# Sums of the down projection moved ahead of the activation's last product on VectorE

## The chip, the core and the metric

The kernel runs on one core of a Trainium2 chip. The metric is the device time of one execution in microseconds (us). TensorE (PE) multiplies matrices into PSUM; VectorE (DVE), ScalarE (ACT) and GpSimd (POOL) work on tiles; SyncE (SP) issues most DMAs. Each engine runs its own instructions strictly in the order in which the program lists them, and semaphores make one wait for another.

## The reference

An attention with a learned bias on relative position feeds a first feed-forward layer with the activation h cos(h), which feeds a second, gated layer behind an RMS norm. Only the first feed-forward layer ("layer 1") matters here:

```python
def _moe_ref(x, w_in, w_out) -> np.ndarray:
    h = x @ w_in              # x: 2304 x 512, w_in: 512 x 2048
    g = h * np.cos(h)
    return (g @ w_out).astype(np.float32)
```

## The kernel before

**Precision.** Every float32 factor of layers 1 and 2 is held as a pair, a rounded first half and a second half with the rest, and `mm3` forms each product from three matmuls (first times first, first times second, second times first). So a weight or an activation is usable only when both halves are written: ScalarE copies the first half, POOL then subtracts it from the value for the second.

**Items.** Layer 1 cuts the 2304 tokens into five blocks `BLKS` (four of 512 and one of 256 columns, block 2) and the 2048 hidden features into 16 groups f of 128. Four groups are one chunk c. An item is one (chunk, block, f); items run chunk by chunk, in a chunk block by block, in a block over its four f. Chunks 0 to 2 take the blocks in the order 0, 1, 2, 3, 4, the last chunk in the order 0, 2, 1, 3, 4. That is 80 items, 20 for each chunk; layer 2 follows with items 80 to 139.

**An item.** `run_item(n)` emits the up product and activation of item n (`item_up`), then the down product of item n-2 (`item_down`, the lag is `LAG`), then `w_tick`. In `item_up` TensorE makes h in one of three PSUM tiles of tag h. VectorE reduces h to the range of the sine (L544 to L546: t, t, r), does half of a weight conversion (`w_fill`: L114 and L115, or L118 and L119), and ScalarE takes the absolute value and the sine of r (L549, L550). VectorE's last step is the product t = r * h (L551); ScalarE copies g's first half from t (L552), POOL makes its second half (L553).

**Down.** `item_down` adds g times the weight into four PSUM tiles y of tag "y", of which there are five. When the last of a block's four f is through (fi == 3), VectorE empties the four tiles into the accumulator `yacc` (`yaccs` for the block of 256 columns): a copy in chunk 0 (L598), a sum later (L600). The next block's down product, one item later, has one spare tile; for its second tile it waits for the first of those four steps.

**Weights.** A weight piece is loaded by DMA, converted from its 64-bit form by VectorE in two halves (`w_fill`), and split into two halves wA or wB by ScalarE (L132) and POOL (L133), in `w_split`. `w_tick` emits at most one split at the end of an item of layer 1, as soon as the buffer's last use has been emitted. The split after item 21 is that of the up weight which item 23 is the first to use; after items 41 and 61 likewise for items 43 and 63.

Of the kernel before, what the change touches and what calls it, by code (L numbers as in the profile page):

```python
# [7 lines left out]
F32 = mybir.dt.float32  # L8
# [3 lines left out]
ALU = mybir.AluOpType  # L12
# [33 lines left out]
def attn_moe(tc, qd, kd, vd, smallp, lrow, ident_d, wf1, wf2, rmsg, out):  # L46
    nc = tc.nc
# [89 lines left out]
    def w_fill(halves=1):  # L137
        for _ in range(halves):
            if wstate["conv"] < wstate["absd"]:
                w_conv()  # L140

    def w_tick(can_split, nsplit=1):

        for _ in range(nsplit):
            i = wstate["split"]
            if i < wstate["convd"] and can_split(i):
                w_split()
        i = wstate["abs"]
        if i < wstate["dmad"] and i < wstate["splitd"] + NW32:
            w_abs()  # L150
        while wstate["dma"] < NP and wstate["dma"] < wstate["conv"] + NRAW:
            w_dma()
        for k in ("dma", "abs", "conv", "split"):
            wstate[k + "d"] = wstate[k]
# [111 lines left out]
    for i, T in enumerate(TORDER):  # L266
# [3 lines left out]
        if nT <= 512 and i % 5 > 1:  # L270
            ps = psA.tile([128, 512], F32, tag="tr", name="psb", bufs=3)
        else:
            ps = psB.tile([128, 1024], F32, tag="S", name="psb", bufs=2)
# [235 lines left out]
    def up(wt, bi, name):  # L509
        t0, tn = BLKS[bi]  # L510
        ps = psH.tile([128, 512], F32, tag="h", name=name, bufs=3)
        mm3(ps[:, :tn],
            [(wt[:, 0, 128 * c:128 * c + 128], wt[:, 1, 128 * c:128 * c + 128],
              xh[:, c, t0:t0 + tn], xl[:, c, t0:t0 + tn]) for c in range(4)],
            tn, True, True)
        return ps
# [3 lines left out]
    def tasks(n, fns):  # L520
        k = 0
        for fn, *a in later.get(n, ()):
            if fn in fns:
                fn(*a)
                k += 1
        return k

    def fill(n):
        return tasks(n, (rms_add, rms_mean, rms_xn))

    def item_up(n):
        m, c, bi, fi = items[n]
        t0, tn = BLKS[bi]
        f = c * (CH1 if m == 1 else CH2) + fi
        g = mp.tile([128, 2, 512], F32R, tag="g", name="g", bufs=LAG + 2)
        if n == 0:

            mp.tile([128, 40], F32, name="even")
        if m == 1:
            ps = up(w_t[(1, f, 0)], bi, "h")[:, :tn]  # L540
            tasks(n, (rms_sum, rms_back))
            t = mp.tile([128, 512], F32, tag="t", name="t", bufs=2)[:, :tn]
            r = mp.tile([128, 512], F32, tag="r", name="r", bufs=2)[:, :tn]
            nc.vector.tensor_scalar(t, ps, INV2PI, MAGIC, op0=ALU.mult, op1=ALU.add)  # L544
            nc.vector.tensor_scalar(t, t, MAGIC, -TWO_PI, op0=ALU.subtract, op1=ALU.mult)  # L545
            nc.vector.tensor_tensor(r, ps, t, op=ALU.add)  # L546
            if fill(n) < WF:
                w_fill()
            nc.scalar.activation(r, r, AF.Abs)  # L549
            nc.scalar.activation(r, r, AF.Sin, bias=halfpi[:, 0:1], scale=-1.0)  # L550
            nc.vector.tensor_tensor(t, r, ps, op=ALU.mult)  # L551
            nc.scalar.copy(g[:, 0, :tn], t)  # L552
            nc.gpsimd.tensor_tensor(g[:, 1, :tn], t, g[:, 0, :tn].bitcast(F32), op=ALU.subtract)  # L553
        else:
            pg = up(w_t[(2, f, 0)], bi, "hg")[:, :tn]
            tasks(n, (rms_sum, rms_back))
            t = mp.tile([128, 512], F32, tag="t", name="t", bufs=2)[:, :tn]
            nc.scalar.activation(t, pg, AF.Sigmoid)  # L558
            nc.vector.tensor_tensor(t, t, pg, op=ALU.mult)  # L559
            fill(n)  # L560
            pv = up(w_t[(2, f, 1)], bi, "hv")[:, :tn]
            nc.vector.tensor_tensor(t, t, pv, op=ALU.mult)  # L562
            nc.scalar.copy(g[:, 0, :tn], t)  # L563
            nc.gpsimd.tensor_tensor(g[:, 1, :tn], t, g[:, 0, :tn].bitcast(F32), op=ALU.subtract)  # L564
        gt[n] = g

    def item_down(n):
        m, c, bi, fi = items[n]
        t0, tn = BLKS[bi]
        ch = CH1 if m == 1 else CH2  # L570
        nch = (NF1 if m == 1 else NF2) // ch
        f = c * ch + fi
        g = gt.pop(n)
        wt = w_t[(m, f, 1 if m == 1 else 2)]
        nd = 4 if m == 1 else tn // 128
        wid = tn if m == 1 else 512
        if fi == 0:
            ypsum[bi] = [env["psY"].tile([128, 512], F32, tag="y", name="y", bufs=5) for _ in range(nd)]
        for d in range(nd):
            ps = ypsum[bi][d][:, :wid]  # L580
            w_ = (wt[:, 0, 128 * d:128 * d + 128], wt[:, 1, 128 * d:128 * d + 128], g[:, 0, :tn], g[:, 1, :tn])
            if m == 1:
                mm3(ps, [w_], tn, fi == 0, fi == ch - 1)
            else:
                gs = slice(128 * d, 128 * d + 128)
                mm3(ps, [(g[:, 0, gs], g[:, 1, gs], wt[:, 0, :], wt[:, 1, :])], 512, fi == 0, fi == ch - 1)
        if fi == ch - 1:
            acc = yacc if m == 1 else oacc
            if c == 0:
                if tn == 512:  # L590
                    acc[bi] = env["yp"].tile([128, 4, 512], F32, tag="y", name="yacc", bufs=4)
                else:
                    acc[bi] = env["yp"].tile([128, nd, wid], F32, tag="ys", name="yaccs", bufs=1)
            a = acc[bi]
            for d in range(nd):
                ps = ypsum[bi][d][:, :wid]
                if c == 0:
                    nc.vector.tensor_copy(a[:, d, :wid], ps)  # L598
                else:
                    nc.vector.tensor_tensor(a[:, d, :wid], ps, a[:, d, :wid], op=ALU.add)  # L600
                if m == 2 and c == nch - 1:
                    nc.sync.dma_start(out[t0 + 128 * d:t0 + 128 * d + 128, :], a[:, d, :])
            if m == 1 and c == nch - 1:
                return bi
        return None
# [63 lines left out]
    def ready(i):  # L669
        while wstate["split"] <= i:  # L670
            if wstate["split"] < wstate["conv"]:
                w_split()
            elif wstate["conv"] < wstate["abs"]:
                w_conv()
            elif wstate["abs"] < wstate["dma"]:
                w_abs()
            else:
                w_dma()

    def run_item(n):  # L680
        tasks(n, (rms_sq, rms_out))
        if n < NI:
            m, c, bi, fi = items[n]
            ready(pieces.index((m, c * (CH1 if m == 1 else CH2) + fi, m - 1)))
            item_up(n)
        d = n - LAG
        if d >= 0:
            m, c, bi, fi = items[d]
            ready(pieces.index((m, c * (CH1 if m == 1 else CH2) + fi, m)))
            bi = item_down(d)  # L690
            if bi is not None:
                n0 = NI1 + RMS_AT[ORDER2.index(bi)]
                for i, x in enumerate(RMS_STEPS):
                    later.setdefault(n0 + i, []).extend((x_[0], bi, *x_[1:]) for x_ in x)
        m, c, bi, fi = items[min(n, NI - 1)]
        w_tick(lambda i: i < WA + WB or lastuse[pieces[i - WA - WB]] <= n - SPL,
               nsplit=2 if n < 6 or m == 2 else 1)
        if m == 2:
            w_fill(2 if n % 2 else 1)
# [6 lines left out]
    for i in range(6):  # L706
        w_split(nc.vector if i % 2 == 0 else nc.gpsimd)
    w_tick(lambda i: False)
    run_item(0)
    av(15, 1, [0, 1, 2, 3, 4])  # L710
    norm_out(15, 1)
    run_item(1)
    st_psA.close()
    st_ap.close()
# [4 lines left out]
    for n in range(2, NI + LAG):  # L719
        run_item(n)  # L720
# [70 lines left out]
```

## Time and profile before

| | us |
|---|---|
| median of 3 runs | 1206.61 (1205.63 to 1207.86) |
| the profiled execution, its own time | 1208.49 |
| its span, first to last instruction | 1206.7 |
| PE busy | 1181.8 (98%) |
| DVE busy | 832.5 (69%) |
| ACT busy | 537.9 (45%) |
| POOL busy | 350.2 (29%) |
| layer 1 up to the turn to layer 2, 350 to 800 us: PE busy | 442.30 of 450.00 |

The granted clock of TensorE is 0.999 of full speed over the span. Matmul ends in the trace are modelled, so a pause of TensorE is best read from the starts before and after it. In a row of the timeline the first number is the start in us from the span's start, the second how long the row lasts; "x4" merges four instructions; a bracket gives the engine's idle time just before and what ended it.

### The profile page before, as it was taken

To read this page: it belongs to the slowest core of one execution; us is meant where nothing else is said; L and a number is where in the kernel's file an instruction comes from. 1 tells how busy PE (TensorE), PEld (TensorE's weight loads), DVE (VectorE), ACT (ScalarE), POOL (GpSimd) and SP (SyncE) were. 2 spreads that over 40 slices of the span, in tenths; PEclk is the share of its full clock that TensorE was granted. 3 is DMA by queue.
4 is the path that set the end of the run, shared out by engine and by line. 5 is a ranking of instruction groups with operands and counts; after the bars stand their busy time and mean duration, and the time that the engine had idled before them with its cause. 6 is when DMAs were issued, how large, how long until landed. Compare 5 with 4: busy or idle time off the path is not lost.

```text
span 1206.7 us, 17433 instructions
## 1 busy us (share of the span) xinstructions
PE 1181.8 (98%) x6596; PEld 907.8 (75%) x6596; DVE 832.5 (69%) x1593; ACT 537.9 (45%) x1073; POOL 350.2 (29%) x356
## 2 busy tenths in 40 slices
PE   7899999999999999999999999999999999999998
PEld 2266666666668888878888877878888888888887
DVE  8866677777669988879878988786456255633232
ACT  6866666666655444445434546422322132222111
POOL 4001011010124234225224445663331242124111
PEclk9999999999999999999999999999999999999999
DMA  5842516343001211201111101111012011200012
GB/s 159 272 158 73 172 34 190 101 133 118 12 1 53 69 37 53 71 18 53 53 35 36 53 18 35 37 53 53 26 45 70 18 35 53 71 1 1 35 43 80
DMA packets 30324, 79.26 MB, mean 66 GB/s; under 512 B 3873, under 2 KB 4129, under 8 KB 30241
## 3 DMA queue, kind: packets, MB, share of 16 engines
q1 hardware_dynamic: 29616, 76.09, 20.1%
q0 software_dynamic: 480, 1.77, 0.6%
q8 instruction: 52, 0.85, 0.3%
q10 hardware_dynamic: 144, 0.29, 0.1%
q14 instruction: 32, 0.25, 0.1%
HBM read 62.52 MB, written 15.61 MB: 65 GB/s over the span
## 4 chain that ended last, share of the span: by engine, by line
PE 84%; DVE 10%; ACT 3%; issue 1%; DMA 1%; POOL 0%; DVEq 0%; ACTq 0%
PE y L506 24%; PE h L506 13%; PE hg L506 11%; PE hv L506 11%; PE o L370 7%; PE psS L313 6%; PE pt L343 5%; PE rp L389 2%; DVE ft L248 2%; PE psS L318 2%; PE psb L277 2%; DVE t L545 1%; DVE yacc L600 1%; PE pt L353 1%; DVE r L546 1%
## 5 line engine op out<-in xcount | busy, mean ns | idle before, releaser
L506 PE MATMUL y<-g,wB 128*128 128x512 f32 (+1 forms) x960 | 214.1, 370 | 5.2 <-DVE yacc L600 1.7
L506 PEld LDWEIGHTS y<-g,wB 128*128 128x128 f32 x960 | 167.7, 188 | 38.7 <-DVE yacc L600 3.0
L553 POOL TENSOR_TENSOR g<-t,g 128x512 fp32r<-128x512 f32 (+1 forms) x80 | 97.4, 1217 | 236.7 <-ACT g L552 236.7
L564 POOL TENSOR_TENSOR g<-t,g 128x512 fp32r<-128x512 f32 (+1 forms) x60 | 74.3, 1239 | 292.1 <-ACT g L563 292.1
L506 PE MATMUL h<-xh,wB 128*128 128x512 f32 (+1 forms) x480 | 145.4, 369 | 0.0
L506 PE MATMUL y<-wB,g 128*128 128x512 f32 x594 | 143.6, 389 | 0.0
L327 DVE CUSTOM_DVE_ANT_0 e<-psS,bias 128x576 f32<-128x576 f32 x144 | 103.7, 754 | 46.5 <-PE psS L313 31.4
L506 PE MATMUL hv<-xh,wB 128*128 128x512 f32 (+1 forms) x440 | 133.6, 369 | 0.0
L506 PE MATMUL hg<-xh,wB 128*128 128x512 f32 (+1 forms) x440 | 133.2, 368 | 0.4 <-DVE t L559 0.4
L559 DVE TENSOR_TENSOR t<-t,hg 128x512 f32<-128x512 f32 (+1 forms) x60 | 38.0, 633 | 137.5 <-ACT t L558 137.5
L331 ACT ACTIVATE e<-e,sm 128x576 f32<-128x576 f32 x144 | 110.6, 769 | 42.9 <-DVE sm L327 42.8
L506 PEld LDWEIGHTS y<-wB,g 128*128 128x128 f32 x594 | 110.8, 188 | 22.5
L558 ACT ACTIVATE t<-hg 128x512 f32<-128x512 f32 (+1 forms) x60 | 33.3, 554 | 168.0 <-PE hg L506 161.7
L563 ACT CAST g<-t 128x512 fp32r<-128x512 f32 (+1 forms) x60 | 34.7, 578 | 164.6 <-DVE t L562 164.6
L549 ACT ACTIVATE r<-r 128x512 f32<-128x512 f32 (+1 forms) x80 | 47.1, 589 | 124.3 <-DVE r L546 123.9
L506 PEld LDWEIGHTS h<-xh,wB 128*128 128x128 f32 x480 | 87.8, 188 | 15.9 <-issue 0.5
L370 PE MATMUL o<-eT,v 128*64 128x256 f32 (+1 forms) x640 | 93.5, 413 | 0.0
L506 PEld LDWEIGHTS hg<-xh,wB 128*128 128x128 f32 x440 | 80.5, 188 | 15.0 <-DVE t L559 0.9
L506 PEld LDWEIGHTS hv<-xh,wB 128*128 128x128 f32 x440 | 80.6, 188 | 13.7
L506 PE MATMUL h<-xl,wB 128*128 128x512 f32 (+1 forms) x240 | 88.4, 368 | 0.0
L133 POOL TENSOR_TENSOR wB<-w,wB 128x512 fp32r<-128x512 f32 x58 | 83.1, 1441 | 0.3 <-ACT wB L132 0.3
L552 ACT CAST g<-t 128x512 fp32r<-128x512 f32 (+1 forms) x80 | 46.2, 578 | 81.3 <-DVE t L551 76.7
(116 smaller groups left out, 2142.7 us busy)
## 6 DMA issues: line engine op xcount, KB each, us to landing
raw<-in_wf_dram SPq DMA_DIRECT2D x68, 512.0 KB, 3.6
bflat<-G SPq DMA_DIRECT2D x36, 295.5 KB, 4.0
bias<-bflat SPq DMA_DIRECT2D x26, 288.0 KB, 2.9
kt<-in_kd_dram SPq DMA_DIRECT2D x16, 320.0 KB, 4.2
qt<-in_qd_dram SPq DMA_DIRECT2D x16, 320.0 KB, 4.5
v<-in_vd_dram SPq DMA_DIRECT2D x16, 320.0 KB, 3.8
out_dram<-yacc SPq DMA_DIRECT2D x16, 256.0 KB, 2.1
bias<-bflat POOLq DMA_DIRECT2D x6, 288.0 KB, 5.7
```

What stands on the lines that cost most here:

```text
L133: eng.tensor_tensor(t[:, 1, :], r, t[:, 0, :].bitcast(F32), op=ALU.subtract)
L313: nc.tensor.matmul(pss[hh][:, x, 0:288], qt_[r, 128 * p:128 * p + 128], kt[r, k0:k0 + 288], start=True, stop=True, tile_position=(64 * hh, 0))
L327: nc.vector.tensor_tensor_reduce(out=e.rearrange("p (a b) -> p a b", a=2), in0=ps[:, :, 0:288], in1=bias_t[j].rearrange("p (a b) -> p a b" ...
L331: nc.scalar.activation(e, e, AF.Exp, bias=s_["m"][:, j:j + 1], scale=-1.0, accum_out=s_["sum"][:, j:j + 1])
L343: nc.tensor.transpose(pt[:, 128 * i:128 * i + 128], e[:, k0:k0 + 128], ident)
L370: nc.tensor.matmul(o[64 * hh:64 * hh + 64, 0:n], vt[:, c, 64 * hh:64 * hh + 64], eT[:, 2 * c + (hh if c < 4 else 0), :], start=(c == 0), s ...
L506: nc.tensor.matmul(ps, a, b_, start=(first and k == 0), stop=(last and k == tot - 1))
L549: nc.scalar.activation(r, r, AF.Abs)
L552: nc.scalar.copy(g[:, 0, :tn], t)
L553: nc.gpsimd.tensor_tensor(g[:, 1, :tn], t, g[:, 0, :tn].bitcast(F32), op=ALU.subtract)
L559: nc.vector.tensor_tensor(t, t, pg, op=ALU.mult)
L564: nc.gpsimd.tensor_tensor(g[:, 1, :tn], t, g[:, 0, :tn].bitcast(F32), op=ALU.subtract)
```

## The change

In layer 1 `item_up` no longer emits the last product and the two steps on g itself. It returns them as a function `rest`, and `run_item` calls it after `item_down`. Layer 2 returns None.

```diff
             nc.scalar.activation(r, r, AF.Sin, bias=halfpi[:, 0:1], scale=-1.0)
-            nc.vector.tensor_tensor(t, r, ps, op=ALU.mult)
-            nc.scalar.copy(g[:, 0, :tn], t)
-            nc.gpsimd.tensor_tensor(g[:, 1, :tn], t, g[:, 0, :tn].bitcast(F32), op=ALU.subtract)
+
+            def rest():
+                nc.vector.tensor_tensor(t, r, ps, op=ALU.mult)
+                nc.scalar.copy(g[:, 0, :tn], t)
+                nc.gpsimd.tensor_tensor(g[:, 1, :tn], t, g[:, 0, :tn].bitcast(F32), op=ALU.subtract)
...
     def run_item(n):
+        rest = None
...
-            item_up(n)
+            rest = item_up(n)
...
             bi = item_down(d)
...
+        if rest is not None:
+            rest()
```

The order differs on VectorE alone, and there at 19 places: the items n = 5, 9, ..., 77, where item n-2 closes a block. TensorE, ScalarE, POOL and SP keep theirs. The lines after the change have moved: L551 is L553, L598 is L602 and L600 is L604.

VectorE at item 33, before: t and r are the activation, w the weight conversion, yaccs the accumulator of the block of 256 columns.

```order
L546 TENSOR_TENSOR r<-h,t 128x512
L114 TENSOR_SCALAR w_5190<-w_5190 128x512
L115 TENSOR_SCALAR w_5190<-w_5190 128x512
L551 TENSOR_TENSOR t<-r,h 128x512
L600 TENSOR_TENSOR yaccs<-y,yaccs 128x256 x4
L544 TENSOR_SCALAR t<-h 128x512
```

VectorE at item 33, after:

```order
L546 TENSOR_TENSOR r<-h,t 128x512
L114 TENSOR_SCALAR w_5190<-w_5190 128x512
L115 TENSOR_SCALAR w_5190<-w_5190 128x512
L604 TENSOR_TENSOR yaccs<-y,yaccs 128x256 x4
L553 TENSOR_TENSOR t<-r,h 128x512
L544 TENSOR_SCALAR t<-h 128x512
```

The four sums now stand between the conversion and the product. VectorE at item 41, before:

```order
L546 TENSOR_TENSOR r<-h,t 128x512
L118 SCALAR_TENSOR_TENSOR w_5521<-raw,w_5521 128x512
L119 SCALAR_TENSOR_TENSOR w_5521<-raw,w_5521 128x512
L551 TENSOR_TENSOR t<-r,h 128x512
L600 TENSOR_TENSOR yacc<-y,yacc 128x512 x4
L544 TENSOR_SCALAR t<-h 128x512
```

VectorE at item 41, after:

```order
L546 TENSOR_TENSOR r<-h,t 128x512
L118 SCALAR_TENSOR_TENSOR w_5521<-raw,w_5521 128x512
L119 SCALAR_TENSOR_TENSOR w_5521<-raw,w_5521 128x512
L604 TENSOR_TENSOR yacc<-y,yacc 128x512 x4
L553 TENSOR_TENSOR t<-r,h 128x512
L544 TENSOR_SCALAR t<-h 128x512
```

The product stands behind the sums here too, and with it whatever waits for the product on other engines.

## Rows read from the trace of the kernel before

**Rows 1.** The page's first part: busy us (share of the span) and instructions.
```profile
PE 1181.8 (98%) x6596; PEld 907.8 (75%) x6596; DVE 832.5 (69%) x1593; ACT 537.9 (45%) x1073; POOL 350.2 (29%) x356
```

**Rows 2.** Timeline (start, us, instruction, idle before), VectorE then TensorE, item 53.
```profile
613.04 0.69 DVE L119 SCALAR_TENSOR_TENSOR w<-raw,w 128x512 int32<-128x512 int32 x1
613.87 0.69 DVE L551 TENSOR_TENSOR t<-r,h 128x512 f32<-128x512 f32 x1
614.48 1.41 DVE L600 TENSOR_TENSOR yaccs<-y,yaccs 128x256 f32<-128x256 f32 x4
...
613.37 0.84 PE L506 MATMUL y<-g,wB 128*128 128x512 f32 x3
614.95 1.42 PE L506 MATMUL y<-g,wB 128*128 128x512 f32 x5 [0.74 <-DVE yaccs L600]
```

**Rows 3.** Timeline of VectorE, POOL and TensorE's weight loads (PEld), item 21.
```profile
456.91 0.69 DVE L551 TENSOR_TENSOR t<-r,h 128x512 f32<-128x512 f32 x1 [0.28 <-ACT r L550]
457.51 2.48 DVE L598 COPY yacc<-y 128x512 f32<-128x512 f32 x4
459.91 0.68 DVE L544 TENSOR_SCALAR t<-h 128x512 f32<-128x512 f32 x1
...
458.45 1.29 POOL L553 TENSOR_TENSOR g<-t,g 128x512 fp32r<-128x512 f32 x1 [2.57 <-ACT g L552]
459.70 1.29 POOL L133 TENSOR_TENSOR wB<-w,wB 128x512 fp32r<-128x512 f32 x1
...
461.21 0.41 PEld L506 LDWEIGHTS h<-xh,wB 128*128 128x128 f32 x2
```

**Rows 4.** Timeline of VectorE, POOL and TensorE's weight loads, item 41.
```profile
557.10 0.68 DVE L551 TENSOR_TENSOR t<-r,h 128x512 f32<-128x512 f32 x1
...
558.63 1.30 POOL L553 TENSOR_TENSOR g<-t,g 128x512 fp32r<-128x512 f32 x1 [2.73 <-ACT g L552]
559.87 1.31 POOL L133 TENSOR_TENSOR wB<-w,wB 128x512 fp32r<-128x512 f32 x1
...
561.23 0.30 PEld L506 LDWEIGHTS h<-xh,wB 128*128 128x128 f32 x2 [0.33 <-POOL wB L133]
```

**Rows 5.** Timeline of POOL in item 22, then in item 42.
```profile
464.99 1.38 POOL L553 TENSOR_TENSOR g<-t,g 128x512 fp32r<-128x512 f32 x1 [4.01 <-ACT g L552]
466.33 1.47 POOL L133 TENSOR_TENSOR wB<-w,wB 128x512 fp32r<-128x512 f32 x1
...
565.18 1.36 POOL L553 TENSOR_TENSOR g<-t,g 128x512 fp32r<-128x512 f32 x1 [4.00 <-ACT g L552]
566.50 1.74 POOL L133 TENSOR_TENSOR wB<-w,wB 128x512 fp32r<-128x512 f32 x1
```

**Rows 6.** Timeline of VectorE, POOL, TensorE's loads and TensorE, items 61 to 65.
```profile
657.09 0.68 DVE L551 TENSOR_TENSOR t<-r,h 128x512 f32<-128x512 f32 x1
664.25 0.68 DVE L544 TENSOR_SCALAR t<-h 128x512 f32<-128x512 f32 x1
677.16 0.41 DVE L551 TENSOR_TENSOR t<-r,h 128x256 f32<-128x256 f32 x1
...
659.89 1.30 POOL L133 TENSOR_TENSOR wA<-w,wA 128x512 fp32r<-128x512 f32 x1
678.20 0.74 POOL L553 TENSOR_TENSOR g<-t,g 128x256 fp32r<-128x256 f32 x1 [1.51 <-ACT g L552]
...
661.24 0.30 PEld L506 LDWEIGHTS h<-xh,wA 128*128 128x128 f32 x2 [0.39 <-POOL wA L133]
...
663.64 1.75 PE L506 MATMUL y<-g,wB 128*128 128x512 f32 x7
678.22 1.82 PE L506 MATMUL y<-g,wB 128*128 128x256 f32 x9 [1.55 <-DVE yacc L600]
681.32 1.60 PE L506 MATMUL y<-g,wB 128*128 128x256 f32 x12
```

**Rows 7.** Timeline of TensorE, item 73.
```profile
718.29 1.89 PE L506 MATMUL y<-g,wB 128*128 128x512 f32 x7 [0.16 <-DVE yacc L600]
```

More of the change, by code (lines that the diff above doesn't have):

```diff
@@ L564, in item_up @@
             nc.gpsimd.tensor_tensor(g[:, 1, :tn], t, g[:, 0, :tn].bitcast(F32), op=ALU.subtract)
+            rest = None
         gt[n] = g
+        return rest
     def item_down(n):
@@ L680, in run_item @@
     def run_item(n):
+        rest = None
         tasks(n, (rms_sq, rms_out))
```

## The prediction

> **What bounds the kernel now.** I read the page's busy times first, then the timeline of layer 1 engine by engine. TensorE is busy for 1181.8 of 1206.7 us [rows 1], so the end moves only by what is added to or taken from TensorE's pauses. The reader should look for two kinds of pause in layer 1, because the change touches both: down multiplications that wait for a PSUM tile which VectorE's sums have still to empty [rows 2, 6], and up multiplications that wait for the second half of a weight which POOL has still to write [rows 4, 6]. The place of the move is the same 19 times: item n with n mod 4 = 1, from item 5 to item 77, where item n-2 closes its block.
>
> **What the move does on VectorE.** It adds and removes no instruction. At each place the product of item n and the four sums change places. The sums may then start as soon as the weight conversion ahead of them is through, so they gain the product's slot (0.61 us for 512 columns) or, where the product was itself waiting for ScalarE, that wait as well. The product starts 2.40 us later than VectorE could have started it: the four sums hold VectorE from 457.51 to 459.91 [rows 3]. The sums' inputs are long there, since the matching down product ended before VectorE arrived, so the sums add no wait of their own.
>
> **Gain: the narrow block (items 13, 33, 53).** The sums of the 256-column block come late for the next block. At item 53 TensorE runs three matmuls into the spare tile from 613.37 and resumes at 614.95. Three such matmuls take 0.84 [rows 2] and seven 1.75 [rows 6], a pitch of 0.91 / 4 = 0.227, so it could have gone on at 613.37 + 3 x 0.227 = 614.05: 0.90 lost. TensorE resumes 0.47 after the first sum starts (614.48 to 614.95). After the change the first sum starts when the conversion is done, 613.04 + 0.61 = 613.65, so TensorE may resume at 614.12 and the loss is 0.07: 0.83 gained [rows 2]. The other two narrow blocks (three such pauses in all, the first at 415.27 and this one the last) show the same two rows; there the product was itself waiting 0.66 for ScalarE, so I count the whole 0.90. Sum: 0.83 + 0.90 + 0.90 = **2.6 us gained**.
>
> **Loss: weights cut just in time (items 21, 41, 61).** The move has a second reach that the diff does not name. The product of item n feeds ScalarE's copy of g and POOL's subtraction of g; the weight split that w_tick issues at the end of the same item (ScalarE L132, POOL L133) stands behind those two on the same two queues. ScalarE and POOL keep their order, so the split slides by as much as the product. In items 21, 41 and 61 that split makes the up weight of the last f of the chunk, used by item n+2's up product right away.
> Item 41: the product started at 557.10 without a wait; POOL took g at 558.63 (1.53 later) and the split from 559.87 to 561.18; TensorE's load of that half came at 561.23, after a pause of 0.33 [rows 4]. It was already the last to arrive. After the change the product starts at 559.50, POOL's g at 561.03.
> How long POOL then needs for the pair is bounded from both sides. Under the sums it took 2.54 (458.45 to 460.99) [rows 3]. Under an item's other VectorE work it took 2.81 in item 22 and 3.06 in item 42 (464.99 to 467.80, 565.18 to 568.24) [rows 5]. After the move the pair no longer runs under the sums but under the next item's work, so I take the longer rows: 2.81 where the next conversion is the first half (L114, L115: items 42 and 62), 3.06 where it is the second (L118, L119: item 22). The split of item 41 then ends at 561.03 + 2.81 = 563.84 and the load comes at 563.89: **2.66 lost**.
> Item 21: VectorE was free at 456.91 - 0.28 = 456.63, so the product moves to 459.03, POOL's g by 2.12 to 460.57, the split's end to 463.63. The load stood at 461.21 and did not wait [rows 3]; it moves to 463.68: **2.47 lost**.
> Item 61: product from 657.09 to 659.49, POOL's g 1.53 later at 661.02, split's end at 663.83, load from 661.24 to 663.88: 2.64 at that point [rows 6]. Part of it meets a stretch in which VectorE, not TensorE, was late. The up product of item 63 was done about 663.64, yet VectorE took it up only at 664.25, with no idle time before. After the change that product is done at 663.64 + 2.64 = 666.28, VectorE waits for it and takes it up by about 666.5 (an estimate, 0.2 for the handover), so VectorE slips by 2.25. At item 65 TensorE waits for the sums (pause of 1.55 before 678.22); they come 0.33 earlier relative to VectorE, hence 678.22 + 2.25 - 0.33 = 680.14. But the product of item 65 goes from 677.16 to 677.16 + 2.25 + 2.40 = 681.81, and POOL's g ends 1.78 after its start (677.16 to 678.94): 683.59, for a down product that stood at 681.32. So **2.3 lost** for items 61 and 65 together; 1.7 if VectorE slips less, 2.64 if nothing is taken back.
> The bound of the three from below is the sums' time alone, with quiet POOL rows: 1.95 + 2.40 + 1.7 = 6.0. From above it is 2.47 + 2.66 + 2.64 = 7.8. I take 2.47 + 2.66 + 2.3 = **7.4 us lost**.
> The Trainium skill, "SBUF — State Buffer", section "Who interferes with whom", has a rule that speaks against this move: VectorE instructions with two SBUF inputs, or in a two-port mode, and GpSimd instructions shut each other out for a whole instruction, while one with at most one SBUF input doesn't. The sums read one SBUF input and one of PSUM, so by that rule they were a free cover for POOL; L545 and the conversion aren't. The rows agree in kind (1.74 for a split beside L118 and L119, 1.29 under the sums). If each of POOL's two steps had to sit out one whole instruction of 0.69 [rows 2] (an estimate from that page's rule), a place would lose 1.4 over the quiet rows instead of 0.27 or 0.52, and the time would be near 1214.
>
> **What costs nothing.** At the other places no split that is soon needed follows the product. g(n) itself is needed by the down product after the next two up products: item 41's g would be written by 562.4 (561.03 + 1.36), while the up product ahead of its use only gets its third weight at 563.89. With 256 columns it is tighter. The nearest row is item 65's: g was ready at 678.94 for a down product at 681.32, 2.38 early against a slip of up to 2.40 [rows 6]. So in items 9, 29 and 49 I count zero and keep 0.3 each for (c). ScalarE's, POOL's and SP's orders and the DMA queues are unchanged. At item 73 the pause of 0.16 (718.29) [rows 7] may go, 0.3 with its drain; VectorE is the late engine again soon after, so I count 0.1 and keep 0.6 for it and items 69 and 77.
>
> **Sum.** Lost 7.4, gained 2.6 + 0.1: +4.7 us on the profiled execution, whose span is 1206.7 and whose own time was 1208.49 (1.8 around the span). The median of the runs shown, 1206.61, lies 1.9 below that; I add the difference to the median: 1206.6 + 4.7 = **1211.3 us**. A measurement of this kernel can tell about 0.2%, 2.4 us, from no change.
>
> **Rivals.**
> (a) The splits arrive in time after all and only the gain is left. This is the faster side: one mechanism, the slack of the three weight halves. It decides at a slack of some 2.2 us at each. For it: at item 21 the load did not wait. Against it: at items 41 and 61 the load did wait, 0.33 and 0.39, on POOL's split [rows 4, 6], so the slack is below zero there, and 0.2 at item 21. Time: 1206.6 - 2.6 to -3.2 = 1203.4 to 1204.0. Chance 0.07.
> (b) The losses are given back in later pauses. Item 65's pause of 1.55 could swallow most of the third loss if VectorE hardly slips. Against it: VectorE's next products are released by the delayed up product itself, so VectorE slips too. With 1.95 and 2.40 for the first two, nothing for the third, and 2.6 to 3.2 gained: 1207.8 to 1208.4; it counts as the same. Chance 0.15.
> (c) The delayed product also holds its PSUM tile of tag h, one of three, 2.4 us longer, and g comes just in time in the narrow items. With another 0.3 at items 9, 29, 49, 65 and 73 and the higher bound of the splits: 1206.6 + 7.8 - 2.6 + 1.5 = 1213.3. For it: the 2.38 against 2.40 above. Against it: it needs all five. Chance 0.10.
>
> **How the numbers follow.** Forecast 0.68 (its own range +2.8 to +5.2, from the bounds 6.0 - 3.2 and 7.8 - 2.6, or 1209.4 to 1211.8), (b) 0.15, (c) 0.10, (a) 0.07. Range 1207.6 to 1213.4: it reaches over most of (b) and all of (c), leaves out (a) and some of (b). Slower by over 0.2%: 0.78; within 0.2%: 0.15; faster: 0.07.
>
> **What would show it.** In the new trace the pauses before 415, 514 and 614 us should be gone, and the up products of items 23, 43 and 63 should each show a pause of two to three microseconds ahead of their third weight load, with POOL's L133 named as what ended it. POOL's pair of steps in items 21, 41 and 61 should take 2.8 to 3.1 instead of 2.5. If those up products flow, I am wrong by (a); if they pause and the time is the same, by (b).

## The result, and the profile after

The changed kernel took 1214.28 us (median of 6 runs, 1213.05 to 1217.26), the kernel before 1207.57 us beside it: a ratio of 1.0057, interval 1.0041 to 1.0074. So it is slower by about 6.7 us, where 4.7 had been forecast and 1213.4 was the upper end of the range. The profiled execution took 1213.64 us with a span of 1211.9. Of all the timed executions one, in the first experiment below, took 2968 us where its others took 1203 to 1207, and no comparison uses it.

The page's first part, after, beside [rows 1] (busy us, share of the span, instructions):

```profile
PE 1186.1 (98%) x6596; PEld 911.3 (75%) x6596; DVE 828.5 (68%) x1593; ACT 537.7 (44%) x1073; POOL 350.1 (29%) x356
```

TensorE issues the same 6596 instructions and is busy 4.3 us longer. A pause ahead of a matmul does not add to busy time; slower matmuls do. That is the first sign of something the forecast had no term for.

What TensorE's weight loads (PEld) waited for between 405 and 780 us, first before, then after (engine, what it loads for, whom it waited for: us in total, times, longest). The lines for the split halves and for the sums stand here:

```profile
PEld y L506 <- DVE yacc L600: 3.0, 5, 1.8
PEld y L506 <- DVE yaccs L600: 2.8, 3, 1.2
...
PEld y L506 <- DVE yaccs L598: 1.2, 1, 1.2
PEld h L506 <- POOL wA L133: 0.4, 1, 0.4
PEld h L506 <- POOL wB L133: 0.3, 1, 0.3
```
```profile
PEld h L506 <- POOL wB L133: 4.4, 2, 2.4
PEld h L506 <- POOL wA L133: 2.1, 1, 2.1
PEld h L506 <- ACT wB L132: 0.8, 2, 0.4
...
PEld y L506 <- DVE yacc L604: 0.5, 3, 0.2
...
PEld y L506 <- DVE yaccs L604: 0.3, 1, 0.3
PEld h L506 <- ACT wA L132: 0.3, 1, 0.3
```

The waits for VectorE's sums shrink from 7.0 to 0.8 us, as intended, and waits for the split halves come in their place: from 0.7 to 6.5 us on POOL, and 1.1 on ScalarE. A load's wait is longer than the pause of the matmuls behind it: the three waits of 2.35, 2.08 and 2.08 us on POOL stand ahead of pauses of TensorE of 1.92, 1.64 and 1.65.

The narrow block, item 53 again (VectorE's timeline of after, beside [rows 2]; start, us, instruction):

```profile
616.34 0.69 DVE L119 SCALAR_TENSOR_TENSOR w<-raw,w 128x512 int32<-128x512 int32 x1
616.94 1.41 DVE L604 TENSOR_TENSOR yaccs<-y,yaccs 128x256 f32<-128x256 f32 x4
618.27 0.68 DVE L553 TENSOR_TENSOR t<-r,h 128x512 f32<-128x512 f32 x1
```

The sums now start when the conversion is done, and the product follows them.

Item 41 and the up product of item 43 (VectorE, POOL, weight loads, TensorE, beside [rows 4]; the bracket is the idle time before and what ended it):

```profile
556.22 2.48 DVE L604 TENSOR_TENSOR yacc<-y,yacc 128x512 f32<-128x512 f32 x4
558.61 0.68 DVE L553 TENSOR_TENSOR t<-r,h 128x512 f32<-128x512 f32 x1
...
560.15 1.35 POOL L555 TENSOR_TENSOR g<-t,g 128x512 fp32r<-128x512 f32 x1 [5.12 <-ACT g L554]
561.47 1.44 POOL L133 TENSOR_TENSOR wB<-w,wB 128x512 fp32r<-128x512 f32 x1
...
562.96 0.30 PEld L506 LDWEIGHTS h<-xh,wB 128*128 128x128 f32 x2 [2.08 <-POOL wB L133]
...
563.52 0.40 PE L506 MATMUL h<-xl,wB 128*128 128x512 f32 x1
564.47 0.63 PE L506 MATMUL h<-xl,wB 128*128 128x512 f32 x1
565.75 0.63 PE L506 MATMUL h<-xl,wB 128*128 128x512 f32 x1
```

The chain is the forecast one: sums, product, g, split, weight load. The load waits 2.08 us instead of 0.33. The last three rows are the new thing: the same matmul takes 0.40 at 563.52 and 0.63 at 564.47 and 565.75, after the pause has ended. The windows of the same stretch say why (columns: window, length, busy of TensorE, weight loads, VectorE, ScalarE, POOL with counts, then the granted clock, DMA share, GB/s; the first line is from before, the others from after):

```profile
562.00:564.00 2.00, 2.00 (x10) 1.60 (x9) 1.31 (x4) 1.35 (x2) 0.00 (x0) 1.00 0.00 0
...
560.00:562.00 2.00, 1.32 (x5) 0.51 (x4) 1.93 (x4) 1.38 (x4) 1.85 (x2) 1.00 0.00 0
562.00:564.00 2.00, 1.04 (x4) 0.86 (x5) 1.79 (x2) 0.62 (x2) 0.90 (x1) 0.98 0.00 0
564.00:566.00 2.00, 2.00 (x6) 1.57 (x5) 0.00 (x0) 1.59 (x3) 1.36 (x2) 0.50 0.00 0
566.00:568.00 2.00, 2.00 (x7) 1.58 (x7) 1.06 (x2) 0.00 (x0) 1.16 (x1) 0.67 0.00 0
```

The granted clock of the changed kernel is 1.00 up to the pause and 0.50 behind it, the lower of TensorE's two levels, 1.2 instead of 2.4 GHz. The same happens behind the other two pauses (0.88, 0.50, 0.77 from 460 to 466; 0.58 and 0.57 from 666 to 670), and in no other 2 us of this trace is it under 0.95. The Trainium skill, "TensorE: Matmul & The Clock Gate", section "Part 1: The HAM clock gate (the "warmup" mystery)", has the clock gate pass half of the pulses in one of its two states and all in the other; the 0.50 agrees.

The two traces compared by the start of each group of matmuls, from layer 1's first to its last, give the account. The change loses 7.4 us in this stretch (end +5.12; the starting point lay at -2.24, ahead of the first changed place, since the attention stage of this execution was that much shorter: in the trace of before the clock fell to 0.71 and 0.50 between 46 and 50 us, in this one it stayed at 1.00 there). That stage differs from run to run, so every comparison below is made from layer 1's start.

### The profile page after: what moved, and what is told of

The parts are those of the page before. It is cut to its first block, busy times and chain, and to the rows that moved or that the text cites. A ratio compares the mean times of both kernels' runs of the same rounds, so it can differ in the third digit from the quotient of the medians.

```text
span 1211.9 us, 17435 instructions
## 1 busy us (share of the span) xinstructions
PE 1186.1 (98%) x6596; PEld 911.3 (75%) x6596; DVE 828.5 (68%) x1593; ACT 537.7 (44%) x1073; POOL 350.1 (29%) x356
## 4 chain that ended last, share of the span: by engine, by line
PE 82%; DVE 12%; ACT 4%; issue 1%; POOL 1%; DMA 1%; DVEq 0%; ACTq 0%; POOLq 0%
PE y L506 22%; PE h L506 12%; PE hg L506 11%; PE hv L506 11%; PE o L370 7%; PE psS L313 6%; PE pt L343 5%; PE rp L389 2%; DVE ft L248 2%; PE psS L318 2%; PE psb L277 1%; DVE yacc L604 1%; DVE t L545 1%; DVE w L118 1%; DVE r L546 1%
## 5 line engine op out<-in xcount | busy, mean ns | idle before, releaser
L313 PE MATMUL psS<-kt,qt 64*128 64x288 f32 x512 | 81.3, 429 | 0.9 <-DVE sm L327 0.6
```

Source lines behind the costliest of these rows:

```text
L313: nc.tensor.matmul(pss[hh][:, x, 0:288], qt_[r, 128 * p:128 * p + 128], kt[r, k0:k0 + 288], start=True, stop=True, tile_position=(64 * hh, 0))
```

## The experiments

Seven further kernels were run, and the changed one again, each timed in several rounds beside the kernel before. "In the stretch" means the shift of layer 1's end against the kernel before, minus that of its start, in the profiled executions, one for each run.

### The split ahead of the product

In items 21, 41 and 61 alone, the weight work of the item is issued ahead of the delayed product, so that neither g nor its subtraction stands ahead of the split on ScalarE and POOL.

```diff
-        if rest is not None:
+        if rest is not None and n not in (21, 41, 61):
             rest()
         m, c, bi, fi = items[min(n, NI - 1)]
         w_tick(...)
+        if rest is not None and n in (21, 41, 61):
+            rest()
```

> The change in full, except that in items 21, 41 and 61 the weight split (and the rest of w_tick) is issued ahead of the late product, so that on ScalarE and POOL it no longer stands behind g. VectorE's order is that of the changed kernel in all 19 places. Theory (the weight halves cut just in time are the whole loss): no pause of over 0.5 us in the up products of items 23, 43 and 63, granted clock 1.00 there, the narrow blocks still gain, 3 to 3.5 us faster than the kernel before. Rival 1 (the loss lies in VectorE's order itself, through late g or late h tiles): still 3 us or more slower than before.

Measured: 1204.51 us, ratio 0.9975, interval 0.9963 to 0.9988: **faster than both kernels**. In the stretch -3.1 us. POOL's order at item 21 (POOL's timeline of this kernel):

```profile
458.19 1.30 POOL L133 TENSOR_TENSOR wB<-w,wB 128x512 fp32r<-128x512 f32 x1 [1.58 <-ACT wB L132]
461.19 1.36 POOL L555 TENSOR_TENSOR g<-t,g 128x512 fp32r<-128x512 f32 x1 [1.71 <-ACT g L554]
```

The split now goes first and ends before 459.5; the waits on L133 vanish from the list of waits. The whole loss hangs on the place of three splits behind three products, and what is left is the gain. That shows where the loss starts, not yet what it consists of.

### Only the three items, and all but the three

```diff
             rest = item_up(n)
+            if rest is not None and not (n in (21, 41, 61)):
+                rest()
+                rest = None
```

> Only items 21, 41 and 61 have the product behind the sums; the other 16 places are as before. Theory: the full loss and none of the gain at the narrow blocks: pauses of 6.3 us in sum (as in the changed kernel's trace), 4.7 us more by the lower clock behind them, less 0.8 us that item 65's wait gives back: about 10 us slower than before. Rival 1 (the loss is spread over all 19 places): 3/19 of 7.4 us, about 1 us.

Measured: 1213.98 us, ratio 1.0058, interval 1.0045 to 1.0071; in the stretch +7.3. The expectation of about 10 was missed. The weight loads of this kernel ahead of the up products of items 23, 43 and 63:

```profile
461.12 0.30 PEld L506 LDWEIGHTS h<-xh,wB 128*128 128x128 f32 x2 [2.36 <-POOL wB L133]
...
563.64 0.50 PEld L506 LDWEIGHTS h<-xh,wB 128*128 128x128 f32 x2 [2.08 <-POOL wB L133]
...
666.90 0.30 PEld L506 LDWEIGHTS h<-xh,wA 128*128 128x128 f32 x2 [2.09 <-POOL wA L133]
```

and the windows behind the three pauses:

```profile
462.00:466.00 4.00, 4.00 (x19) 3.30 (x18) 2.35 (x4) 1.14 (x2) 2.53 (x2) 1.00 0.44 135
562.00:566.00 4.00, 2.36 (x7) 1.87 (x7) 2.44 (x3) 2.60 (x5) 2.27 (x3) 0.68 0.00 0
666.00:670.00 4.00, 3.10 (x14) 2.56 (x15) 2.14 (x3) 2.15 (x4) 2.27 (x3) 1.00 0.00 0
```

The pauses came at all three places; the clock fell behind one of them only. Two of the three terms of 1.6 us were missing, which is most of the difference from 10. Two smaller ones nearly cancel: the splits themselves cost 1.1 more than in the changed kernel (2.3, 2.5 and 2.6 without the clock), and 0.9 came back at the narrow block of item 53. So the lower clock may follow such a pause and need not.

The converse, the other 16 places alone (the same edit with `n not in (21, 41, 61)`):

> The other half: 16 places changed, items 21, 41 and 61 as before. Theory: only the gain of the three narrow blocks is left, 2.9 us by the changed kernel's trace, with up to 0.5 us more at items 65 to 77: 2.9 to 3.4 us faster than before. Rival 1: 16/19 of the loss, about 6 us slower.

Measured: 1204.01 us, ratio 0.9977, interval 0.9966 to 0.9988; -2.9 in the stretch. The gain is there by itself, and the two halves (+7.3 and -2.9) add up to 4.4, where the whole lost 7.4. Two drops of the clock fewer are worth 3.1 of that; the splits' dearer terms and the 0.9 given back at item 53 nearly cancel.

### Only the narrow blocks

The same edit with `n in (13, 33, 53)`.

> Only the three items that close the narrow blocks (13, 33, 53) get the new order; the other 16 places have the order of before. If the gain of the change lies in the three narrow blocks alone: the pauses of 0.7 to 0.75 us there go, nothing else changes, the time is 2.6 to 2.9 us under before (ratio 0.9976 to 0.9978) and equals that of the kernel with all places but 21, 41 and 61. If part of that kernel's gain came from the other 13 places: 1 to 2 us under before.

Measured: 1203.25 us, ratio 0.998, interval 0.9969 to 0.9991. Ahead of item 65's pause its trace was 3.1 us ahead of before (-2.47 against +0.61 at layer 1's start). So all of the gain that can be measured comes from three of the 19 places. This profile brought something else, at item 65, where the pause for VectorE's sums is still there (TensorE's row, and the windows behind it):

```profile
675.61 1.10 PE L506 MATMUL y<-g,wB 128*128 128x256 f32 x5 [1.42 <-DVE yacc L604]
```
```profile
676.00:678.00 2.00, 2.00 (x12) 1.64 (x12) 1.97 (x5) 0.82 (x2) 0.33 (x1) 0.82 0.59 229
678.00:680.00 2.00, 2.00 (x11) 2.00 (x10) 1.61 (x5) 0.93 (x2) 0.00 (x0) 0.50 0.00 0
680.00:682.00 2.00, 2.00 (x14) 1.96 (x14) 1.83 (x4) 1.98 (x5) 0.75 (x1) 0.82 0.00 0
```

A pause at another place, for another engine, is followed by the same drop, at an item that keeps the order of before. So the lower clock needs neither the splits nor the new order. In the kernel before, the pause of 1.55 at that very place [rows 6] was not followed by one:

```profile
678.00:680.00 2.00, 1.78 (x11) 1.42 (x12) 2.00 (x5) 1.29 (x3) 0.74 (x1) 1.00 0.76 223
```

Three more of the kernels here pause at that place, for 1.22 or 1.23 us, and their clock stays at 1.00: one drop behind five such pauses.

### Work in the pause

After the change, with eight extra matmuls into the same PSUM tile ahead of the up products of items 23, 43 and 63; the up product's own first matmul overwrites what they write. The pause is filled, the wait for the weight stays.

```diff
-            ps = up(w_t[(1, f, 0)], bi, "h")[:, :tn]
+            ps = up(w_t[(1, f, 0)], bi, "h", 8 if n in (23, 43, 63) else 0)[:, :tn]
...
+        for _ in range(fill):
+            nc.tensor.matmul(ps[:, :tn], wt[:, 0, 0:128], xh[:, 0, t0:t0 + tn], start=True, stop=True)
```

> The changed kernel with eight extra matmuls of 512 columns ahead of the first matmul of the up products of items 23, 43 and 63. They read the weight's first half, which is there early, and write to the same h tile, which the first real matmul then starts anew. They last 8 x 0.227 = 1.8 us and lie inside the pause of 1.9 to 2.6 us. Theory (TensorE's clock falls because it stood still): granted clock 1.00 behind the pause, so the 4.7 us go and 2.7 us against before are left. Rival 2 (the matmuls behind the pause are slow for another reason, as ScalarE's and POOL's work beside them): they stay at 0.43 us apart, and the time stays 7 us above before, or more where the extra matmuls stick out.

Measured: 1212.77 us (1208.79 to 1214.7), ratio 1.0041, interval 1.0025 to 1.0057; in the stretch **+3.2**. Weight loads and windows at item 43:

```profile
563.63 0.19 PEld L506 LDWEIGHTS h<-xh,wB 128*128 128x128 f32 x1
564.32 0.30 PEld L506 LDWEIGHTS h<-xh,wB 128*128 128x128 f32 x2 [0.27 <-POOL wB L133]
```
```profile
562.00:564.00 2.00, 2.00 (x10) 1.65 (x10) 1.97 (x3) 1.36 (x2) 2.00 (x2) 1.00 0.00 0
564.00:566.00 2.00, 2.00 (x10) 1.47 (x9) 1.15 (x2) 0.76 (x2) 0.27 (x2) 1.00 0.00 0
```

The weight halves come as late as before, the clock stays at 1.00 at all three places, and the loss is less than half. In the stretch, 24 matmuls of useless work make the changed kernel 4.2 us shorter than in its first profile, and 2.8 shorter than in its second (below).

The medians of the timed runs point the same way and differ by less (1212.8 against 1214.3, with intervals that overlap): in some executions the clock also falls far from the change, in this profile within the first 60 us. Its two runs with a mean clock of 1.00 took 1208.79 and 1209.19. The clock can be taken out of every timed run by counting its span times its mean clock (an estimate: the clock is given to 0.001, some 1.2 us, and TensorE is taken to bound the whole span). The medians are then 1208.8 and 1209.6 for the two sets of runs of the changed kernel, 1209.4 with the pauses filled, 1209.8 with them half filled (next), and 1206.2 to 1206.5 before: without the lower clock the changed kernel and the filled ones are level, some 3 us above before.

Four extra matmuls instead of eight leave about half of the pause.

> The changed kernel with 4 instead of 8 extra matmuls (128 rows by 512 columns, about 0.21 us each) ahead of the up products of items 23, 43 and 63, whose results are overwritten. The waits for the weight's second half get shorter by 0.85 us and become 1.2 to 1.5 us; the up products end when they did, since the weights come no earlier. If the length of the pause decides: the clock stays at 1.00 behind all three, and the loss in the stretch is +2.7 to +3.3 us, as with 8. If any pause there brings the clock down: +4.3 to +7.9 us with the clock at 0.5 to 0.7 in the two to four microseconds behind them.

Measured: 1211.79 us, ratio 1.0041, interval 1.0029 to 1.0053; in the stretch +3.1. Weight load and windows at item 43:

```profile
563.09 0.30 PEld L506 LDWEIGHTS h<-xh,wB 128*128 128x128 f32 x2 [1.18 <-POOL wB L133]
```
```profile
562.00:564.00 2.00, 1.25 (x6) 0.78 (x5) 1.92 (x2) 0.61 (x1) 1.04 (x1) 1.00 0.00 0
564.00:566.00 2.00, 2.00 (x11) 1.62 (x10) 0.22 (x1) 1.71 (x3) 1.23 (x1) 1.00 0.00 0
```

Loads that waited 1.18 to 1.44 us were followed by a clock of 1.00 at all three places. The loss is that of the full filling, as expected if the weights set the end and the clock is not touched.

### The changed kernel again

> The changed kernel once more, for a second profile of it. Theory: the three pauses of 2.1 to 2.4 us ahead of the up products of items 23, 43 and 63 come again with the same lengths to 0.1 us, the narrow blocks flow, and the loss inside the changed stretch is 2.7 us plus about 1.57 us for each of the three pauses after which the granted clock falls to 0.5 (0 to 3 of them, so +2.7 to +7.4). Rival (the matmuls behind the pauses are slow for a reason of the order itself): the same lower clock at the same three places every time, +7.4.

Measured: 1214.74 us, ratio 1.0065, interval 1.0053 to 1.0077; in the stretch +6.0. Weight loads ahead of the up products of items 23 and 43, and the windows behind them:

```profile
463.07 0.30 PEld L506 LDWEIGHTS h<-xh,wB 128*128 128x128 f32 x2 [2.36 <-POOL wB L133]
...
563.86 0.30 PEld L506 LDWEIGHTS h<-xh,wB 128*128 128x128 f32 x2 [2.09 <-POOL wB L133]
```
```profile
462.00:464.00 2.00, 0.93 (x4) 0.80 (x5) 2.00 (x2) 0.34 (x1) 1.02 (x1) 1.00 0.00 0
464.00:466.00 2.00, 2.00 (x11) 1.64 (x10) 0.42 (x2) 1.14 (x2) 0.99 (x1) 1.00 0.62 174
564.00:566.00 2.00, 2.00 (x6) 1.55 (x7) 0.69 (x2) 1.22 (x3) 0.46 (x1) 0.54 0.00 0
566.00:568.00 2.00, 2.00 (x7) 1.58 (x6) 0.00 (x0) 0.49 (x1) 2.00 (x2) 0.60 0.00 0
```

The same program at the same place (item 23): after a wait of 2.35 us the clock fell in the first profile, after 2.36 it did not in this one. Behind item 63's pause it fell again (0.64 and 0.50 from 666 to 670). The rival, that the order itself makes the matmuls slow each time, falls. Two drops of three fit the +6.0 (2.7 + 2 x 1.57 = 5.8).

### The split first at all 19 places

The first experiment's edit with `n % 4 == 1` for the three numbers.

> At all 19 places (items n with n mod 4 = 1) the weight work that the item issues goes ahead of the delayed product on VectorE, ScalarE and POOL, not at 21, 41 and 61 alone. At the other 16 places no weight is needed soon, so nothing is gained there; the product and g come later by the conversion, 0.6 to 1.2 us. Theory: where g has that slack the time is that of the kernel with items 21, 41 and 61 alone, some 3 us under before (ratio 0.997 to 0.998). Rival: in the narrow items (9, 29, 49) and at 65 g comes too late for its down product, pauses of 0.3 to 1.2 us there, ratio 0.998 to 1.001.

Measured: 1204.57 us, ratio 0.998, interval 0.9969 to 0.9992; -2.6 in the stretch. It is level with the version that treats three items (1204.51): the later products of the other places cost nothing that the timed runs can tell. In the stretch it is 0.5 behind that version, and of the rival's pauses a small one came: a weight load of item 49's down product waits 0.21 for POOL's g, which it does not do there. Waits of 0.28 to 0.29 at items 9 and 65 stand in both.

## Why the prediction was right and wrong

The mechanism, the places and the sign were as forecast; the size was not. Of the 3.0 us between 1211.3 and 1214.28, 1.0 is the base: the kernel before had a median of 1206.61 in the three runs that the forecast adds to, and 1207.57 in the six beside the result. The rest is in the terms, read in the profiled executions (+7.4 there). The terms, from the group starts, in us. The second column is the kernel with the filled pauses, where the clock stays up; the half-filled one gives the same for the three splits (2.51, 1.86, 1.84). The up products of items 23, 43 and 63 came 4.14, 3.42 and 3.42 later in the changed kernel; what exceeds the second column there stands as its clock term, so that this term is a difference:

| term | forecast | filled, clock at 1.00 | changed kernel |
|---|---|---|---|
| narrow blocks, items 13, 33, 53 | -2.6 | -2.9 | -2.9 |
| split of item 21 | +2.47 | +2.57 | +2.57 |
| split of item 41 | +2.66 | +1.87 | +1.87 |
| split of item 61 | +2.64 | +1.83 | +1.83 |
| given back, item 65 and behind | -0.4 | -0.3 | -0.8 |
| lower clock behind the three pauses | none | none | +4.7 |
| sum (steps under 0.12 are left out) | +4.7 | +3.1 | +7.3 |

**The step that failed** is the price of a pause. The prediction put a late weight at the time by which it is late. It took for granted that the matmuls behind the pause run as fast as those before; the three windows with 0.50 say they don't. The term was 0 and measured 4.7, about 1.6 for each drop. The windows give about the same size on their own: at item 43 the clock lacks 0.02, 0.50 and 0.33 of three stretches of 2 us, together 1.7 us of work, and the windows behind the other two pauses lack as much. The trace of before gave no warning: behind the pause of 1.55 of [rows 6], the longest in layer 1, the granted clock is 1.00. One pause without a drop is no evidence that there is none; item 65 of the kernel with only the narrow blocks moved shows a drop at that very place.

**Part of that error was covered** by one of the other sign: items 41 and 61 slipped by 1.9 and 1.8, not by 2.66 and 2.64. The forecast left VectorE's arrival at the sums where it stood. In the changed kernel it came 0.7 earlier, and the whole of it is one instruction, L545 of the item ahead (VectorE and POOL, before, then after):

```profile
553.51 1.23 DVE L545 TENSOR_SCALAR t<-t 128x512 f32<-128x512 f32 x1
553.17 1.30 POOL L553 TENSOR_TENSOR g<-t,g 128x512 fp32r<-128x512 f32 x1 [2.57 <-ACT g L552]
```
```profile
553.36 0.52 DVE L545 TENSOR_SCALAR t<-t 128x512 f32<-128x512 f32 x1
552.30 1.30 POOL L555 TENSOR_TENSOR g<-t,g 128x512 fp32r<-128x512 f32 x1 [2.57 <-ACT g L554]
```

In both, L545 ends 0.27 to 0.28 after POOL's subtraction of g does (554.74 after 554.47, 553.88 after 553.60). It starts soon after POOL in the one and near POOL's end in the other, so it takes 1.23 or 0.52. With only the three items moved (second experiment) L545 takes 1.24 at that place, and the slip there is 4.06 with the drop behind it, near 2.5 without, as the forecast said; so the term was right for that order of events, and the other places' moves put POOL's g ahead. This is read from the rows; no run changed L545 alone, and what in the chain from one place to the next brings POOL forward was not followed up. In the second profile of the changed kernel, L545 ahead of item 61 takes 1.21 again, and the load's wait for ScalarE grows from 0.3 to 1.0.

**Point by point.** The narrow blocks: the last of them gained 0.83 as forecast (1.04 in the kernels whose splits are not late), the other two 1.04 and 1.05, for which 0.90 was put; together right. The product's place behind the sums, the split's slide behind g, L133 as the releaser at three up products: right. POOL's pair: 2.76 in items 41 and 61 and 3.03 in item 21 (457.46 to 460.49), forecast 2.81 and 3.06; the whole excluded instruction of 0.69 for each step, priced at 1.4 a place, did not come for POOL. It is VectorE's L545 in the rows above that ends only after POOL's instruction. The Trainium skill, "SBUF — State Buffer", section "Who interferes with whom", names tensor_scalar, the kind of L545, among the VectorE instructions that can enter a mode in which they and GpSimd's shut each other out for a whole instruction. These rows agree for VectorE, though no run shows the mode; POOL's pair, 0.2 to 0.5 longer than under the sums, does not show it. Item 65: the pause of 1.55 went and 0.3 was given back with the clock up; in the changed kernel another 0.5, probably since slower matmuls give VectorE time (not tested). There g of item 65 came late by 0.33, as the forecast's estimate had it:

```profile
686.06 1.13 PEld L506 LDWEIGHTS y<-g,wB 128*128 128x128 f32 x9 [0.33 <-POOL g L555]
```

**The rivals.** (a), splits in time, needed 2.2 us of slack and found none; the first experiment shows that it would have given 1204.5 if the split did not stand behind the product. (b), losses given back, fell: 0.3 to 0.8 came back of 6.3. (c), g and the h tile late, had the nearest time of the three (1213.3) for a wrong reason: of its five places only items 9 and 65 showed a late g, 0.29 and 0.33, and at item 9 a wait for the sums went in exchange. The estimate of 1214, with whole instructions lost by POOL, lay nearer still, and that is luck: the loss it names did not come.

What stays open is when the clock falls. Behind the nine loads that waited 2.08 us or more in the two profiles of the changed kernel and in the second experiment, it fell six times.

## What to carry to other kernels

A moved producer takes with it everything that stands behind its consumers on their own queues: follow each consumer's engine one item further and ask who waits for what comes next there. Here the fix was to issue the split first at three items, which kept the gain and dropped the loss (1204.5 against 1206.8 before and 1214.3). When a change puts a pause like these into dense work of TensorE (1.6 to 1.9 us between matmuls), count its length and, as an upper end, the 1.6 us more that a drop of the clock cost here; if the pause can't be removed, harmless matmuls in it can be cheaper than the pause.

## What the hardware showed unexpectedly

- Waits of TensorE's weight loads of 2.08 to 2.36 us between dense matmuls (1.64 to 1.92 from matmul to matmul) were followed by a granted clock of 0.50 in six of nine cases, at a cost of some 1.6 us each; those of 1.18 to 1.44 us in the half-filled kernel in none of three. But at item 65 a pause between matmuls of 1.42 us was followed by a drop in one kernel, and one of 1.55 at the same place in another was not.
- The same program at the same place did both: 2.35 us with a drop, 2.36 without.
- VectorE's L545 takes 0.43 alone and 1.23 beside POOL's g; at the places shown it ended 0.27 to 0.28 after POOL's instruction. VectorE's arrival at item 41's sums moved by 0.7 with it.
